# Second-layer products of a soft mixture of experts: four column groups of TensorE per piece in place of two

## The chip, the cores and the metric

The kernel runs on one core of a Trainium2 chip. The metric is the device time of one execution in microseconds. Before the change it is 203.27 us, the median of three runs (203.27 to 203.29).

## The reference

Eight batches of eight heads (576 positions, head dimension 64) pass through an attention with 32 memory slots. The result is laid out as a matrix x of 4608 rows and 512 columns, which goes through a soft mixture of experts with 8 experts of 4 slots each:

```python
logits = x @ phi                                   # 4608 x 32
d = softmax(logits, over rows);  slot_input = d.T @ x     # 32 x 512
for e in range(8):                                 # 4 slots each
    h = maximum(slot_input[e] @ w1[e], 0)          # 4 x 1024
    slot_out[e] = h @ w2[e]                        # 4 x 512
c = softmax(logits, over columns)
out = c @ slot_out                                 # 4608 x 512, float32
```

The weights w1 and w2 are 16.8 MB each, and the output is 9.4 MB. All of it is float32.

## The kernel before

The kernel has two parts. The first, up to about 137 us, does the attention batch by batch, and the logits and the sums of x under their softmax on the way; x itself is never stored. The second part does the experts and writes the output. A planner (the class Plan) takes every group of instructions with a cost in microseconds, a priority and its tiles, simulates the engines and writes out one order for each engine's queue. The order is fixed when the kernel is built; on the chip each engine waits on semaphores only.

**The experts' first layer** (`expert_in`, L1376): for each expert two loads of 1 MB, and 32-column weights (the slot inputs) against 256 columns of w1, put at four positions of the array, `tile_position=(0, NS * j)` with j from 0 to 3 (L1385). `hidden` turns the hidden values round; `hT()[:, x, ...]` then holds them for TensorE's weights, 32 columns per expert of which only its own four are not zero, so that all experts add up in one 32-row block.

**The second layer** (`expert_out` L1439, `mult` L1425): the output's 512 columns are done in two halves, d = 0 and d = 1, each with a bank of PSUM of its own: `pacc[0]` lies in kvbank, `pacc[1]` in scbank. w2 of an expert is laid with eight rows in each partition, and a piece h (0 or 1) is four of them. One call of `mult` does one piece for one half d: four products, each a 32-column weight taken from `hT()[:, 4 * k + x, ...]` against 256 columns of one of the four rows:

```python
for k in range(2):
    for x in range(2 * h, 2 * h + 2):
        nc.tensor.matmul(dst[NS * x: NS * x + NS, :HD], ..., tile_position=(0, NS * x))
```

NS is 32, so x is the column group of the array and also the 32-row block of PSUM in which the product is added. Piece 0 uses groups 0 and 1, piece 1 groups 2 and 3. A float32 product is two instructions (with a weight load each), so that one call of `mult` is 8 matmuls and 8 weight loads. There are 16 pieces and two halves, 32 calls, 256 matmuls. The four blocks of PSUM are four partial sums; `slot_sums` (L1345) copies the bank out (L1349), adds the four blocks with one product against `rep` (L1357), and writes the result `sr` in two parts (L1364, L1369).

**The last five pieces** (the `tails`: piece 1 of expert 5, and both of experts 6 and 7) are loaded apart. `tail_out` (L1471) issues ten loads of 256 KB for the half d = 0 and then ten for d = 1, two for each piece and half. So the half d = 0 is finished while the other's weights are still on their way:

```python
tail_mult(0, n)        # five pieces, half 0, then slot_sums(0)
direct(0, i)           # two output blocks of half 0, before cT is needed
half_group(0, n, ...)  # 16 more blocks of half 0; between them the five tail_mult(1, m)
slot_sums(1), direct(1, i), half_group(1, n), then blocks of both halves
```

Each output block is a product into one of four PSUM banks (L1602; L1586 for the direct ones), a copy out by VectorE (L1579) or ScalarE (L1578), and a store. Stores (L1615) and loads (L502) are all issued by SyncE's queue, in the planner's order: the stores come behind the last load. A store takes one block (128 KB), a group of three (384 KB) or, at the end, 3, 6 and 9 blocks of full width (768, 1536 and 2304 KB). The planner's cost for a call of `mult` is 0.45 us, and it is written as a number where the call is added.

Of the kernel before, what the change touches and what calls it, by code (L numbers as in the profile page):

```python
# [270 lines left out]
def kernel(  # L271
# [27 lines left out]
    E, DM, FF = w1.shape  # L299
    NS = moe_phi.shape[1]  # L300
# [1030 lines left out]
    hT = lambda: hTb.ap.rearrange("p (x y) -> p x y", x=8)  # L1331
# [8 lines left out]
    HD = DM // 2  # L1340
# [4 lines left out]
    def slot_sums(d, middle=lambda: None):  # L1345
        x = slice(d * HD, d * HD + HD)
        add(
            *((ACT, act(HD)) if d else (DVE, dve(HD))),
            lambda: (nc.scalar.copy if d else nc.vector.tensor_copy)(  # L1349
                accs.ap[:, x], pacc[d].ap[:, 0, :HD]  # L1350
            ),
            r=[pacc[d]], w=[accs.part(d)],
        )
        y = middle()
        z = add(
            PE, 0.5,
            lambda: nc.tensor.matmul(  # L1357
                so[d].ap[:, :HD], rep.rearrange("p a n -> p (a n)"), accs.ap[:, x],
                start=True, stop=True,
            ),  # L1360
            r=[accs.part(d), rep_b], w=[so[d]], after=[y] if y is not None else (),
        )
        add(
            ACT, act(HD), lambda: nc.scalar.copy(sr.ap[:, 0, x], so[d].ap[:, :HD]),  # L1364
            r=[so[d]], w=[sr.part(d)],
        )
        add(
            DVE, dve(HD),
            lambda: nc.vector.tensor_tensor(  # L1369
                sr.ap[:, 1, x], so[d].ap[:, :HD], sr.ap[:, 0, x].bitcast(F32), op=ALU.subtract  # L1370
            ),
            r=[so[d], sr.part(d)], w=[sr.part(d)],
        )
        return z
# [50 lines left out]
    def mult(dst, e, h, t, d):  # L1425
        n = 2 if e < ONES else 4
        wide = t.ap.rearrange("p (j t d) -> p j t d", j=n, t=2)
        for k in range(2):
            for x in range(2 * h, 2 * h + 2):
                nc.tensor.matmul(  # L1430
                    dst[NS * x: NS * x + NS, :HD],
                    hT()[:, 4 * k + x, NS * e: NS * e + NS],
                    wide[:, x % n, k, d * HD: d * HD + HD],
                    start=(e == 0 and k == 0),
                    stop=(e == E - 1 and k == 1),
                    tile_position=(0, NS * x),
                )

    def expert_out(e):  # L1439
        w2v = w2[e].rearrange("(p x) d -> p (x d)", x=8)  # L1440
        if e < ONES:
            for h in range(2):
                t = load_w(w2v[:, h * W_SZ: h * W_SZ + W_SZ])
                for d in range(2):
                    add(
                        PE, (0.45, 16),
                        lambda d=d, h=h, t=t: mult(pacc[d].ap[:, 0], e, h, t, d),
                        r=[hTb.part(e // EG), t], w=[pacc[d]],
                    )
            return  # L1450
# [9 lines left out]
        for h in range(2):  # L1460
            if h not in whole:
                tails.append((e, h, t))
                continue
            for d in range(2):
                add(
                    PE, (0.45, 16),
                    lambda d=d, h=h: mult(pacc[d].ap[:, 0], e, h, t, d),
                    r=[hTb.part(e // EG), *(t.part(4 * h + i) for i in range(4))], w=[pacc[d]],
                )
# [13 lines left out]
    def tail_mult(d, n, after=()):  # L1483
        e, h, t = tails[n]
        return add(
            PE, (0.45, 16), lambda: mult(pacc[d].ap[:, 0], e, h, t, d),
            r=[hTb.part(e // EG), *(t.part(4 * h + 2 * d + i) for i in range(2))],
            w=[pacc[d]], after=after,
        )
# [92 lines left out]
    def direct(d, i, after=()):  # L1582
        po, ot, s = b_o.tile(), half[0], slice(d * HD, d * HD + HD)
        x = add(
            PE, 0.45,
            lambda: nc.tensor.matmul(  # L1586
                po.ap[:, :HD], c4.ap[:, i * P: i * P + P], accs.ap[:, s],
                start=True, stop=True,
            ),
            r=[accs.part(d), c4], w=[po], also=[ot], after=after,  # L1590
        )
        add(
            *evict(lambda: ot.ap[:, i * DM + s.start: i * DM + s.stop], po, HD, i % 2 == d),
            r=[po], w=[ot.part(G * d + i)],
        )
        store(0, i, s, ot, [ot.part(G * d + i)], i)
        return x
# [47 lines left out]
    for n in range(-1, NA):  # L1645
# [5 lines left out]
        if RIGHT[NT - 1] == n:  # L1651
            y = slot_sums(1)
            for i in range(ND):
                y = direct(1, i, [y])
# [47 lines left out]
```

## Time and profile before

| what | value |
|---|---|
| median of three runs | 203.27 us |
| the profiled execution | 203.85 us |
| its span, first to last instruction | 202.1 us |
| mean granted clock of TensorE | 0.967 |
| TensorE busy | 171.5 us (85%) |
| VectorE, ScalarE, GpSimd busy | 141.0, 74.7, 95.6 us |
| DMA | 76.47 MB, mean 378 GB/s |
| L1430 (the products of `mult`), kvbank / scbank | 15.1 / 15.5 us busy, 128 matmuls each |

The profile is that of one execution, which took 203.85 us; 1.75 us of it lie outside the span. PE is TensorE's matmuls and PEld its weight loads, DVE is VectorE, ACT ScalarE, POOL GpSimd, SPq the queue of SyncE that issues the DMAs. Times in rows are microseconds from the start of the span, durations in the tables by line are nanoseconds. Ends of matmuls are modelled, and two that overlap are both counted from start to end.

### The profile page before, as it was taken

To read this page: it belongs to the slowest core of one execution; us is meant where nothing else is said; L and a number is where in the kernel's file an instruction comes from. 1 tells how busy PE (TensorE), PEld (TensorE's weight loads), DVE (VectorE), ACT (ScalarE), POOL (GpSimd) and SP (SyncE) were. 2 spreads that over 40 slices of the span, in tenths; PEclk is the share of its full clock that TensorE was granted. 3 is DMA by queue.
4 is the path that set the end of the run, shared out by engine and by line. 5 is a ranking of instruction groups with operands and counts; after the bars stand their busy time and mean duration, and the time that the engine had idled before them with its cause. 6 is when DMAs were issued, how large, how long until landed. Compare 5 with 4: busy or idle time off the path is not lost.

```text
span 202.1 us, 6096 instructions
## 1 busy us (share of the span) xinstructions
PE 171.5 (85%) x2607; PEld 110.2 (55%) x2607; DVE 141.0 (70%) x267; ACT 74.7 (37%) x191; POOL 95.6 (47%) x92
## 2 busy tenths in 40 slices
PE   7889748978789899798999788899999998999910
PEld 6667535545557386465575356565555653557500
DVE  6831640499899899999899996478999502448820
ACT  2022314526361755607373252100347301246600
POOL 7199203479994994799944284000036920000000
PEclk9999996699999999999999999999999999999985
DMA  6999999999999999999999999999999999689996
GB/s 198 363 395 391 383 385 389 383 388 381 401 360 390 385 385 402 381 399 399 417 412 418 417 420 422 420 420 438 425 415 407 342 335 331 224 299 301 393 431 292
DMA packets 31642, 76.47 MB, mean 378 GB/s; under 512 B 2048, under 2 KB 15872, under 8 KB 28288
## 3 DMA queue, kind: packets, MB, share of 16 engines
q1 hardware_dynamic: 31616, 76.09, 99.3%
q8 instruction: 20, 0.33, 0.7%
q14 instruction: 6, 0.05, 0.1%
HBM read 66.65 MB, written 9.44 MB: 377 GB/s over the span
## 4 chain that ended last, share of the span: by engine, by line
PE 38%; DMA 20%; POOL 16%; DVE 10%; issue 6%; SPq 4%; ACT 2%; POOLq 0%; DVEq 0%
DMA arena<-in_moe_w_dram 12%; DMA arena<-in_v_dram 8%; PE bank L1602 7%; PE scbank L813 5%; PE kvbank L704 4%; POOL arena L669 4%; POOL arena L871 4%; SPq L502 4%; PE bank L882 4%; POOL arena L848 4%; PE bank L1385 3%; POOL arena L648 3%; PE scbank L1430 2%; PE bank L1010 2%; DVE arena L827 1%
## 5 line engine op out<-in xcount | busy, mean ns | idle before, releaser
L648 POOL TENSOR_TENSOR arena<-arena 128x1152 f32<-128x1152 f32 x8 | 21.0, 2632 | 16.4 <-ACT arena L641 14.1
L591 DVE STREAM_TRANSPOSE arena<-top 128x1152 f32<-128x1152 f32 x16 | 21.6, 1355 | 8.5 <-DMA top<-in_q_dram 8.5
L704 PE MATMUL kvbank<-arena 64*32 64x128 f32 x1152 | 20.6, 273 | 6.4 <-issue 2.6
L520 PE MATMUL kvbank<-ones 128*128 128x256 f32 x82 | 23.2, 419 | 2.4 <-ACT arena L728 1.3
L813 PE MATMUL scbank<-arena 64*64 64x288 f32 x256 | 23.4, 440 | 2.0 <-DVE arena L827 2.0
L669 POOL TENSOR_TENSOR arena<-arena 128x128 f32<-128x128 f32 (+2 forms) x32 | 23.4, 731 | 3.2 <-ACT arena L657 1.3
L1540 POOL TENSOR_TENSOR cT<-cS,cT 32x640 fp32r<-32x640 f32 (+1 forms) x8 | 11.3, 1413 | 26.2 <-ACT cT L1535 25.8
L871 POOL TENSOR_TENSOR arena<-arena,ssm 128x576 f32<-128x576 f32 x16 | 18.3, 1152 | 10.0 <-DVE ssm L867 7.9
L848 POOL TENSOR_TENSOR arena<-arena,smx 128x576 f32<-128x576 f32 x16 | 18.4, 1153 | 8.1 <-DVE smx L843 8.1
L704 PEld LDWEIGHTS kvbank<-arena 64*32 64x32 f32 x1152 | 16.1, 105 | 10.7 <-issue 5.5
L606 DVE TENSOR_REDUCE arena<-arena 128x128 f32<-128x1152 f32 x8 | 17.1, 2152 | 4.4 <-DMA arena<-in_phi_dram 4.4
L882 PE MATMUL bank<-arena 128*128 128x288 f32 x64 | 18.6, 423 | 1.0 <-DVE arena L874 0.8
L1579 DVE COPY arena<-bank 128x256 f32<-128x256 f32 (+1 forms) x30 | 14.4, 510 | 7.0 <-PE bank L1602 6.4
L520 PEld LDWEIGHTS kvbank<-ones 128*128 128x128 f32 x82 | 15.6, 205 | 5.9 <-ACT arena L728 1.7
L827 DVE STREAM_TRANSPOSE arena<-scbank 128x576 f32<-128x576 f32 x16 | 12.3, 766 | 6.7 <-PE scbank L813 6.7
L1602 PE MATMUL bank<-sr,cT 64*128 64x256 f32 (+1 forms) x100 | 15.1, 358 | 0.5 <-ACT arena L1578 0.2
L1430 PE MATMUL scbank<-arena 128*32 128x256 f32 x128 | 15.5, 381 | 0.0
L1430 PE MATMUL kvbank<-arena 128*32 128x256 f32 x128 | 15.1, 384 | 0.4 <-DMA arena<-in_moe_w_dram 0.2
L813 PEld LDWEIGHTS scbank<-arena 64*64 64x64 f32 x256 | 9.8, 141 | 10.0 <-DVE arena L827 3.3
L853 ACT ACTIVATE arena<-arena 128x576 f32<-128x576 f32 x16 | 10.9, 684 | 10.2 <-POOL arena L848 10.0
L882 PEld LDWEIGHTS bank<-arena 128*128 128x128 f32 x64 | 11.2, 189 | 5.9 <-issue 1.7
L1578 ACT COPY arena<-bank 128x256 f32<-128x256 f32 (+1 forms) x24 | 10.4, 445 | 9.9 <-PE bank L1602 9.0
(135 smaller groups left out, 271.3 us busy)
## 6 DMA issues: line engine op xcount, KB each, us to landing
arena<-in_moe_w_dram SPq DMA_DIRECT2D x19, 1024.0 KB, 14.0
top<-in_q_dram SPq DMA_DIRECT2D x8, 1152.0 KB, 11.6
arena<-in_k_dram SPq DMA_DIRECT2D x8, 1152.0 KB, 10.4
arena<-in_v_dram SPq DMA_DIRECT2D x8, 1152.0 KB, 12.9
arena<-in_moe_w_dram SPq DMA_DIRECT2D x3, 2048.0 KB, 14.2
arena<-in_moe_w_dram SPq DMA_DIRECT2D x20, 256.0 KB, 6.1
arena<-in_phi_dram SPq DMA_DIRECT2D x8, 576.0 KB, 7.2
out_dram<-arena SPq DMA_DIRECT2D x10, 384.0 KB, 4.0
```

The lines of the kernel that those rows point to most:

```text
L520: lambda: nc.tensor.matmul(warm.ap, ones, ones.unsqueeze(1).to_broadcast([P, 2, P]), start=True, stop=True,),
L591: lambda: nc.vector.transpose(qT.ap.rearrange("p (i u y) -> p u i y", i=2, y=Y), qt.ap[:, h * QT_SZ: h * QT_SZ + QT_SZ].rearrange("p (u i ...
L606: lambda: nc.vector.tensor_reduce(mx.ap[:, c0:c1], ph().rearrange("p c j m -> p c m j"), axis=AX.X, op=ALU.max),
L648: lambda: nc.gpsimd.tensor_tensor(ph(), ph(), mb.ap[:, c0:c1].unsqueeze(2).to_broadcast([P, c1 - c0, J, M]), op=ALU.subtract,),
L669: plus = lambda o, x, y: nc.gpsimd.tensor_tensor(o, x, y, op=ALU.add)
L704: nc.tensor.matmul(acc.ap[M * c: M * c + M, a, : 2 * D], ph()[h0: h0 + HALF, c, j, :], kv()[h0: h0 + HALF, :, c, j * D: j * D + D], start= ...
L813: nc.tensor.matmul(scb.ap[HALF * g: HALF * g + HALF, a, :JY], pair[g].kd.ap[h0: h0 + HALF, i, c].rearrange("p r m -> p (r m)"), pair[g].qT ...
L848: lambda: nc.gpsimd.tensor_tensor(exv(), exv(), bc(mx), op=ALU.subtract),
L871: lambda: nc.gpsimd.tensor_tensor(exv(), exv(), bc(sm), op=ALU.mult),
L882: nc.tensor.matmul(lp.ap[:, :JY], vpb.ap[:, h, :], aT.ap[:, a * JY: (a + 1) * JY], start=(h == 0), stop=(h == H - 1),)
L1430: nc.tensor.matmul(dst[NS * x: NS * x + NS, :HD], hT()[:, 4 * k + x, NS * e: NS * e + NS], wide[:, x % n, k, d * HD: d * HD + HD], start=( ...
L1602: nc.tensor.matmul(po.ap[:, : x.stop - x.start], cT[bp].ap[y: y + HALF, j // 2 * P: j // 2 * P + P], sr.ap[y: y + HALF, t, x], start=(t == 0),
```

## The change

In `mult` the two loops exchange the roles of the column groups. The column group is now x = 2k + j, and the piece's own index is y = 2h + j, which still picks the weights and the row of w2. So the four products of one call go to the four groups 0, 1, 2, 3, whatever the piece, where before they went to 0, 1, 0, 1 (piece 0) or 2, 3, 2, 3 (piece 1). Every product, its operands, and the order of the calls stay the same; only the block of PSUM to which a product is added differs, and `slot_sums` adds the blocks as before. The flags that begin and end an accumulation move from k to h, since each block is now met first by piece 0 of expert 0 and last by piece 1 of expert 7.

```diff
         for k in range(2):
-            for x in range(2 * h, 2 * h + 2):
+            for j in range(2):
+                x, y = 2 * k + j, 2 * h + j
                 nc.tensor.matmul(
                     dst[NS * x: NS * x + NS, :HD],
-                    hT()[:, 4 * k + x, NS * e: NS * e + NS],
-                    wide[:, x % n, k, d * HD: d * HD + HD],
-                    start=(e == 0 and k == 0),
-                    stop=(e == E - 1 and k == 1),
+                    hT()[:, 4 * k + y, NS * e: NS * e + NS],
+                    wide[:, y % n, k, d * HD: d * HD + HD],
+                    start=(e == 0 and h == 0),
+                    stop=(e == E - 1 and h == 1),
                     tile_position=(0, NS * x),
                 )
```

## Rows read from the trace of the kernel before

**Rows 1.** By stretch: length; busy PE, PEld, DVE, ACT, POOL; clock, DMA share, GB/s.

```profile
160.00:168.00 8.00, 7.62 (x110) 4.08 (x103) 0.00 (x0) 0.23 (x1) 3.00 (x3) 1.00 1.02 332
168.00:173.00 5.00, 4.48 (x34) 2.51 (x32) 1.97 (x5) 1.39 (x4) 0.00 (x0) 1.00 1.01 330
173.00:184.00 11.00, 10.74 (x84) 6.55 (x81) 5.87 (x16) 4.29 (x12) 0.00 (x0) 1.00 0.74 249
184.00:200.50 16.50, 8.27 (x46) 5.06 (x45) 7.74 (x14) 5.82 (x11) 0.00 (x0) 0.85 1.02 402
```

**Rows 2.** Chain that ended last, from 161 us: start, length, what.

```profile
161.55 6.13 DMA arena<-in_moe_w_dram
167.72 1.06 PE kvbank L1430 x6
...
170.85 0.99 PE scbank L1430 x8
...
172.52 0.99 PE scbank L1430 x8
...
173.93 0.99 PE scbank L1430 x8
...
177.97 0.99 PE scbank L1430 x8
...
192.55 0.69 DVE arena L1579
```

**Rows 3.** SyncE's DMA issues: ten last loads; one store; the last store.

```profile
L502 SPq DMA_DIRECT2D arena<-in_moe_w_dram x10: 368/368/1365, 162.2 to 169.2; - x10
DMA to landing us min/median/max: 5.4/5.6/6.2
...
L1615 SPq DMA_DIRECT2D out_dram<-arena x1: 383/383/383, 175.9 to 175.9; - x1
...
L1615 SPq DMA_DIRECT2D out_dram<-arena x1: 333/333/333, 193.3 to 193.3; - x1
DMA to landing us min/median/max: 7.9/7.9/7.9
```

**Rows 4.** TensorE in order of time: start, length, operation, count.

```profile
136.86 7.06 PEld L1385 LDWEIGHTS bank<-arena,SIM 128*32 128x32 f32 x128 [0.61 <-DVE SIM L1264]
145.65 1.13 PE L1385 MATMUL bank<-top,SIM 128*32 128x256 f32 x16
157.20 0.39 PE L1430 MATMUL scbank<-arena 128*32 128x256 f32 x2
157.24 0.39 PE L1430 MATMUL kvbank<-arena 128*32 128x256 f32 x2
157.42 0.39 PE L1430 MATMUL scbank<-arena 128*32 128x256 f32 x2
170.78 1.06 PE L1430 MATMUL scbank<-arena 128*32 128x256 f32 x8
```

**Rows 5.** Line L1430 alone: one weight load, ns min/median/max.

```profile
L1430 PEld LDWEIGHTS kvbank<-arena x128: 106/109/110, 151.9 to 168.2; 128*32 128x32 f32 x128
```

**Rows 6.** DMA in half microseconds: length, clock, DMA share, GB/s.

```profile
175.50:176.00 0.50, 1.00 0.12 41
...
176.50:177.00 0.50, 1.00 0.29 102
```

**Rows 7.** Granted clock early in the span; columns as in rows 1.

```profile
28.30:30.80 2.50, 0.00 (x0) 0.00 (x0) 1.83 (x1) 0.00 (x0) 0.00 (x0) 1.00 1.05 388
31.75:38.50 6.75, 6.30 (x42) 3.75 (x45) 1.83 (x3) 3.73 (x10) 2.62 (x1) 0.50 1.07 384
54.70:56.00 1.30, 0.19 (x2) 0.10 (x1) 1.06 (x4) 1.14 (x4) 1.30 (x2) 1.00 0.98 336
```

**Rows 8.** Chain of waits: one group of L813 at either clock; columns as in rows 2.

```profile
34.16 2.69 PE scbank L813 x15
...
65.29 1.18 PE scbank L813 x16
```

## The prediction

> **What bounds the kernel now.** I read three views in this order: busy time by stretch, for which stage is short of what; the chain that ended last, for what holds the end; and TensorE's instructions in order of time, for what one call of `mult` costs.
>
> By stretch [rows 1], the DMA engines are full from 160 to 173 us (shares 1.02 and 1.01) and again from 184 to 200.5 (1.02). Between them, from 173 to 184, their share is 0.74, and there TensorE is busy for 10.74 of 11 us. So this is the one late stretch in which TensorE, and not the transfers, sets the pace: the weights have arrived, and the output blocks are not yet made fast enough to fill the engines.
>
> The chain [rows 2] says the same. A load ends its wait at 167.7; then comes the rest of the last piece of half 0 (six matmuls, 1.06 us), and five times a whole call for half 1 with 0.99 us each, of which the first three and the last stand in the rows, among the output blocks. The chain ends with a copy at 192.55, behind which the last store is issued at 193.3 and lands 7.9 us later [rows 3]: it moves 2.3 MB and queues behind what is still under way. So the end is TensorE's pace before 184 us and a full queue after it.
>
> **What a call costs, before and after.** A call is 8 matmuls. Alone on the array, on two column groups, it takes 1.06 us from first start to last end, and the work behind it starts 0.99 us after it [rows 2, 4]. On one column group, matmuls follow each other every 0.215 us: a pair of scbank starts at 157.20 and the next pair at 157.42 [rows 4]. The call puts four on each of its two groups, so it lasts four such rounds.
>
> Four groups can run at once: between those two starts a pair for kvbank starts at 157.24, and it belongs to the next piece, on the other two groups, so that 4 matmuls pass in 0.215 us [rows 4]. The first layer, which uses all four groups in its inner loop, does 16 matmuls, also four rounds, in 1.13 us [rows 4]. After the change a call is two rounds on four groups. Two rounds less than the first layer's 16 are 1.13 - 2 x 0.215 = 0.70 us; two rounds less than today's call are 1.06 - 0.43 = 0.63. The saving of a call that stands alone is thus 0.36 to 0.43 us. I take 0.40, the middle; the rows allow nothing below zero, since each group gets fewer matmuls and their number is the same.
>
> A weight load takes 0.109 us [rows 5]. The Trainium skill, "TensorE: Matmul & The Clock Gate", section "Part 3: Packing small matmuls — row/col tiling", says that a weight load overlaps matmuls in flight only when their row groups differ; here all use all rows. By that rule eight loads would stand one behind the other, a call would not go below its present length, and the time would stay. This case's trace speaks against it: 128 weight loads of the first layer, all of them on all rows, took 7.06 us together, where end to end they would have taken 14.
>
> **Where the saving counts.** There are 32 calls.
>
> 1. The 22 calls of the first eleven pieces (both halves, about 152 to 164 us) mostly overlap already, as the rows at 157 us show: consecutive pieces use different groups. They gain little, perhaps 1 us at the places where two calls with the same groups meet. All of it is lost again in the wait for the last weights: the engines are full up to 173 us whatever TensorE does, and the last load of half 0 ends its wait at 167.7 [rows 1, 2]. Cost and gain at the end: none. If a piece were late behind its data, the wait at 167.7 would not stand in the chain.
>
> 2. The last call of half 0. Two matmuls run when the first of its two loads has landed, six after the second. Today these are four on one group and two on the other, so four rounds. After it they are two on each of three groups, so two rounds: 0.40 us on the chain, between the load and the copy L1349.
>
> 3. The five calls of half 1 that stand in the chain, each between output products that use all columns and can't overlap with it: 5 x 0.40 = 2.0 us.
>
> Half 1's weights must not be late instead. Ten loads issued from 162.2 to 169.2 land within 5.4 to 6.2 us [rows 3], the last at about 174.7; they are evenly spaced by some 0.8 us, so the pairs are complete at about 169, 170.5, 172, 173.3 and 174.7. The first three calls and the last start today at 170.85, 172.52, 173.93 and 177.97 by the chain [rows 2], and by the sum above they would start 0.40, 0.80, 1.20 and 2.00 us earlier: at 170.4, 171.7, 172.7 and 176.0. The nearest margin is that of the third, 0.7 us. The copies out of PSUM don't become the bound either: from 173 to 184 us VectorE is busy for 5.87 and ScalarE for 4.29 of 11 us [rows 1], and would be so in about 9.
>
> Sum on TensorE: 6 x 0.40 = 2.4 us earlier from the first block of half 1 on (bounds 6 x 0.36 = 2.2 and 6 x 0.43 = 2.6). All later copies and the issues of the stores move with it, and the last store would be issued at 190.9 in place of 193.3.
>
> **What the queue of stores makes of it.** From 184 us on the engines are full, so issuing earlier helps only as far as the engines have holes before. Against the full share of 1.02 the 11 us at 0.74 hold 11 x (1 - 0.74 / 1.02) = 3.0 us of holes. The largest lies between 175.5 and 177 us (shares 0.12 and 0.29 in its first and last half microsecond), before the bytes of the store issued at 175.9 [rows 3, 6]: a start-up of about 1 us. Behind three calls of half 1 and the last of half 0, that store is issued 1.6 us earlier, at 174.3, and its bytes start at about 175.3, when those before it end. The stores of half 0 that follow come 1.6 to 2.4 us earlier and leave no hole. The first three of half 1 are single blocks of 128 KB (0.4 us each at the 330 GB/s of rows 1) issued some 0.5 us apart, and leave some 0.5 us of holes. So about 3.0 - 0.5 = 2.5 us of engine time are won, while TensorE gives 2.4: two limits near each other, each of them of a sum with holes in it. When I follow the stores one by one, with a fixed time from the last byte to the landing, I get 2.0. I take 2.2 us.
>
> The profiled execution would end at 203.85 - 2.2 = 201.65 us (its span at 199.9); it stands 0.58 us above the median, so the median would be 203.27 - 2.2 = 201.1 us. The case's own range is 200.7 (2.6 us, TensorE's upper bound) to 201.6 (1.7 us).
>
> **The rivals.**
>
> A. The holes are not the late stores' but the engines' own, or the first stores get in each other's way: the bytes then start late after an earlier issue as well, and only the part after 177 us is won, 3.0 less the 1.2 us of the large hole and 0.6 for the rest, some 1.2 us. Time: 202.1. For it: the engines are idle at 175.5 to 177, though the store before it, of half 0 too, had been issued when its bytes could follow the loads at once. Against it: the hole ends 1 us after an issue.
>
> B. The four groups don't run at once here, because two of the four products now share neither weights nor rows of w2 (in the first layer, four groups share one weight); a call keeps its four rounds, as by the skill's rule above. Time: 203.3. Against it: the overlap at 157 us is between just such products.
>
> C. The slower side: the clock. Faster calls leave TensorE waiting for the last weights of half 0, from about 162.5 to 168 us. With five calls of 0.65 us spread over these waits it is busy for some 60%, against 7.62 of 8 us today [rows 1]. Early in the span the granted clock fell from 1.00 to 0.50, that is from 2.4 to 1.2 GHz, after 2.5 us without a matmul, and then stayed there for 6.75 us [rows 7]; the same group of L813 took 2.69 us in it and 1.18 us at full clock [rows 8]. Such a fall at 168 us would cost about half of the low stretch, 3.4 us, against the 2.4 won: 1.0 us later, 204.3. [...]
>
> **How the numbers follow.** Forecast 0.72, A 0.15, B 0.07, C 0.06. The range reaches from 200.6, just past TensorE's bound, to 202.5, which takes in A and leaves out B and C (0.13) and the edges. A measurement of this kernel tells 0.2% (0.4 us) from no change. Faster: the forecast and A, 0.87. Same: B, 0.07. Slower: C, 0.06.
>
> **What would show it.** In the profile after, a call of half 1 standing alone takes 0.63 to 0.70 us in place of 1.06 (if it is 1.0, B); the chain has 0.55 to 0.65 us for each in place of 0.99; the copy L1349 of half 0 starts near 168.4 and the last store is issued near 190.9 (if these hold and the end moves by much less, A); the share of the DMA engines from 173 to 182 us rises from 0.74 to above 0.9; the clock stays at 1.00 until the last product (if not, C). The prediction is wrong as a whole if the weights of half 1 are waited for, which I have at 0.7 us of margin, or if the output blocks turn out to wait for their copies.

## The result and the profile after

The changed kernel takes 200.94 us (median of four runs, 200.49 to 201.16) against 203.28 us for the kernel before, run beside it. The ratio is 0.9877, with a 95% interval of 0.9855 to 0.9899. Later, on another occasion, the two stood at 200.89 and 203.27 us (0.9883, 0.9867 to 0.9899). The change saves 2.3 us; 2.2 us and 201.1 us were forecast.

Of the two profiled executions, the one before took 203.85 us, 0.57 above its median, and the one after 200.49, 0.45 below. They lie 3.4 us apart, so about 1 us between these two traces is not the change, and below it is kept apart.

The chain that ended last, of the kernel after, from 161 us; its rows answer to [rows 2]. Line 1430 of the kernel before is now 1431, 1602 is 1603.

```profile
161.25 5.52 DMA arena<-in_moe_w_dram
166.77 0.04 issue
166.81 0.67 PE kvbank L1431 x6
...
169.54 0.57 PE scbank L1431 x8
170.11 0.67 PE bank L1603 x8
170.78 0.57 PE scbank L1431 x8
...
171.78 0.57 PE scbank L1431 x8
...
173.74 0.57 PE scbank L1431 x8
...
174.99 0.61 PE scbank L1431 x8
...
189.17 0.69 DVE arena L1580
```

The chain passes through the same instructions, but for one step: behind the last call of half 1 it now goes through the copy L1349 (0.38 us) where it went through four output products (0.43). Its last call of half 0 is 0.67 us long where it was 1.06; the five calls of half 1 are four times 0.57 and once 0.61 where they were 0.99. That is 0.39 and 4 x 0.42 + 0.38 = 2.06 us, together 2.45. The last copy begins at 189.17 in place of 192.55, 3.38 us earlier: 2.45 from the six calls, and 0.91 because the last load of half 0 ended its wait at 166.77 in this execution, where it did at 167.68 in the other.

A second profiled execution of the changed kernel (the run after_again below) took 200.93 us, close to its median. There the load ended its wait at 167.24, and the last copy begins 2.91 us earlier than before, 0.44 of it from the load and 2.47 from the calls:

```profile
161.74 5.50 DMA arena<-in_moe_w_dram
...
189.64 0.69 DVE arena L1580
```

TensorE in order of time, of the kernel after: one call of half 1, and the products that follow it.

```profile
169.47 0.64 PE L1431 MATMUL scbank<-arena 128*32 128x256 f32 x8
170.04 0.39 PE L1603 MATMUL bank<-sr,cT 64*128 64x256 f32 x2
```

The call lasts 0.64 us from first start to last end, against 1.06 [rows 4]: two rounds of 0.215 less, 0.63, was the lower of the two estimates.

Busy time by stretch, of the kernel after; the columns are those of [rows 1].

```profile
160.00:168.00 8.00, 7.07 (x77) 2.42 (x69) 0.42 (x1) 0.00 (x0) 2.71 (x2) 1.00 0.97 316
168.00:173.00 5.00, 5.00 (x48) 2.87 (x48) 2.17 (x6) 1.57 (x5) 0.00 (x0) 1.00 1.07 351
173.00:184.00 11.00, 10.64 (x84) 7.28 (x84) 7.82 (x19) 6.39 (x17) 0.00 (x0) 1.00 1.01 344
```

From 173 to 184 us the share of the DMA engines has risen from 0.74 to 1.01. In this execution the holes are gone but for one at 176.5 to 177 us:

```profile
176.50:177.00 0.50, 1.00 0.60 207
```

The second execution has more of them. Its share is 0.98, which against the full 1.02 leaves 11 x (1 - 0.98 / 1.02) = 0.4 us of holes:

```profile
173.00:184.00 11.00, 10.63 (x86) 7.40 (x86) 7.66 (x19) 6.28 (x17) 0.00 (x0) 1.00 0.98 329
```

And the last store, of which the kernel before has its row in [rows 3], of the kernel after:

```profile
L1616 SPq DMA_DIRECT2D out_dram<-arena x1: 333/333/333, 189.9 to 189.9; - x1
DMA to landing us min/median/max: 8.0/8.0/8.0
```

It is issued 3.4 us earlier and waits and moves for 8.0 us where it took 7.9, so the end moves by as much as TensorE did.

### The profile page after: what moved, and what is told of

It reads as the page before. It is cut to its first block, busy times and chain, and to the rows that moved or that the text cites. A ratio compares the mean times of both kernels' runs of the same rounds, so it can differ in the third digit from the quotient of the medians.

```text
span 198.7 us, 6096 instructions
## 1 busy us (share of the span) xinstructions
PE 168.9 (85%) x2607; PEld 107.7 (54%) x2607; DVE 141.5 (71%) x267; ACT 74.4 (37%) x191; POOL 95.5 (48%) x92
## 4 chain that ended last, share of the span: by engine, by line
PE 37%; DMA 20%; DVE 14%; POOL 12%; issue 4%; SPq 4%; ACT 3%; DVEq 0%; POOLq 0%
DMA arena<-in_moe_w_dram 12%; DMA arena<-in_v_dram 9%; PE bank L1603 6%; PE scbank L813 6%; PE kvbank L704 5%; PE bank L882 4%; SPq L502 4%; POOL arena L848 3%; PE bank L1385 3%; POOL arena L871 3%; POOL arena L669 3%; POOL arena L648 3%; PE bank L1010 2%; DVE arena L606 2%; DVE arena L827 2%
## 5 line engine op out<-in xcount | busy, mean ns | idle before, releaser
L813 PE MATMUL scbank<-arena 64*64 64x288 f32 x256 | 23.6, 445 | 2.3 <-DVE arena L827 2.3
L813 PEld LDWEIGHTS scbank<-arena 64*64 64x64 f32 x256 | 10.0, 141 | 10.1 <-DVE arena L827 3.7
L1603 PEld LDWEIGHTS bank<-sr,cT 64*128 64x128 f32 x100 | 9.9, 184 | 6.5 <-DVE arena L1580 4.1
L1385 PE MATMUL bank<-arena,SIM 128*32 128x256 f32 x224 | 13.3, 392 | 0.2 <-DVE SIM L1264 0.2
```

What stands on the lines that cost most here:

```text
L813: nc.tensor.matmul(scb.ap[HALF * g: HALF * g + HALF, a, :JY], pair[g].kd.ap[h0: h0 + HALF, i, c].rearrange("p r m -> p (r m)"), pair[g].qT ...
L1385: nc.tensor.matmul(hb.ap[NS * j: NS * j + NS, :256], SIM.ap[:, 2 * i + c, NS * e: NS * e + NS], wv[:, c].rearrange("p (x j t) -> p x j t", ...
L1603: nc.tensor.matmul(po.ap[:, : x.stop - x.start], cT[bp].ap[y: y + HALF, j // 2 * P: j // 2 * P + P], sr.ap[y: y + HALF, t, x], start=(t == 0),
```

## The experiments

All times are medians beside runs of the kernel before on the same chip; ratios are to that kernel.

**Where the saving counts.** Four kernels use the four column groups in some of the calls only, and the old two in the others. They differ in one condition, and the flags that begin and end an accumulation follow it:

```diff
+        new = 2 * e + h >= 2 * E - NT and d == 1     # half1_only: five calls
+        new = 2 * e + h >= 2 * E - NT and d == 0     # half0_only: five calls
+        new = 2 * e + h < 2 * E - NT                 # main_only: the 22 others
+        new = 2 * e + h >= 2 * E - NT                # tails_only: ten calls
...
+                y = 2 * h + j
+                x = 2 * k + j if new else y
```

> Only the five calls of half 1 that stand between the output blocks use four column groups; the other 27 are as before. By the theory (each of them is 0.4 us shorter on the chain, and the holes of the store queue take it up): five times 0.42, about 2.1 us faster than before, 201.2. By the rival that a part of the gain comes from the earlier stage (in the profile after, the wait for the last load of half 0 ends 0.9 us earlier): not more than 1.5 us, 201.8 or later.

Measured: 201.44 us against 203.35, ratio 0.992 (0.9901 to 0.9938). The gain is 1.9 us by the medians and 1.6 (1.3 to 2.0) by the ratio. It is somewhat under the 2.1 expected, and the interval does not quite reach that; it takes in the rival's 1.5 as well, so this run alone does not decide between them, but most of the gain is here.

> Only the five calls of half 0 for the last five pieces use four column groups. By the theory only the last of them is on the chain: 0.4 us faster than before, 202.9. By the rival of the earlier stage: 0.4 and whatever comes with an earlier last load, up to 1.3 us, 202.0.

Measured: 202.91 us against 203.35, ratio 0.9981 (0.9973 to 0.999): 0.4 us, as the one call on the chain predicts.

> Only the 22 calls of the first eleven pieces use four column groups; the ten calls of the last five pieces are as before. By the theory the transfers set this stage: no change, 203.3, and the last load of half 0 ends its wait where it did. By the rival of the earlier stage: 0.9 us faster, 202.4.

Measured: 203.30 us against 203.35, ratio 0.9999 (0.999 to 1.0009). Twenty-two of the 32 calls, changed alone, are worth nothing. In the chain of this kernel the wait for a load still stands before the last call of half 0:

```profile
161.54 5.62 DMA arena<-in_moe_w_dram
167.17 0.04 issue
167.21 1.06 PE kvbank L1433 x6
```

The rival's 0.9 us is outside the interval of this run (0.2 us either way). The three gains by medians are 1.9, 0.4 and 0.05 us and add up to 2.4, against 2.3 for all calls at once.

Whether the 22 calls matter once the ten later ones are short was then tried by the counterpart, beside the kernel after.

> Only the ten calls of the last five pieces (both halves) use four column groups; the 22 earlier calls are as before. By the theory (the earlier stage waits for its weights either way): as the kernel after on the same chip, within 0.2 us. By the rival that the earlier calls matter once the later ones are short (in two profiles with the earlier calls as before, the chain ran through TensorE from 160 us on, without a wait for a load): 0.3 to 0.5 us slower than the kernel after.

> The kernel after, unchanged, timed beside tails_only on the same chip: 200.9 by both theories, 2.0 to 2.5 us less than the kernel before.

Measured: tails_only 200.99 us, ratio 0.9888 (0.9871 to 0.9906); the kernel after 200.89, ratio 0.9883 (0.9867 to 0.9899); before 203.27. There is no difference that can be told: the ten calls do all of it, as far as 0.2 us can be told.

**How much the store queue lets through.** Two kernels leave out the five calls of half 1 for the last five pieces, before and after the change, and keep everything else in its place (the flags that end an accumulation follow). What TensorE no longer does there is 5 x 0.99 and 5 x 0.57 us.

```diff
     def mult(dst, e, h, t, d):
+        if d == 1 and 2 * e + h >= 2 * E - NT:
+            return
```

> The kernel before, with the five calls of half 1 for the last five pieces left out (their share of the output's right half is missing); loads, order and stores stay. TensorE gets 5 x 0.99 = 4.95 us. By the theory of two limits the holes of the store queue (3.0 us) cap the gain: 2.5 to 3.0 us, 200.3 to 200.8, with the DMA share full from 173 us on. By the rival that TensorE alone sets the end: 4.95 us, 198.3.

Measured: 201.05 us against 203.35, ratio 0.99 (0.9879 to 0.9921): 2.3 us by medians, 1.6 to 2.5 by the interval, out of TensorE's 4.95. TensorE alone is refuted, and the cap stands somewhat lower than the 2.5 to 3.0 us expected.

> The kernel after, with the five calls of half 1 for the last five pieces left out (their share of the output's right half is missing); loads, order and stores stay. TensorE gets another 5 x 0.57 = 2.85 us. By the theory that the store queue is now full (holes of some 0.3 us are left from 173 us on): at most 0.3 us faster than the kernel after, 200.6 to 200.9. By the rival that TensorE still sets the end: 2.85 us faster than it, 198.1.

Measured: 200.48 us against 203.44, ratio 0.9832 (0.978 to 0.9884). That is 0.4 us less than the kernel after in its own runs (200.89 and 200.94, on other occasions), for 2.85 us less work. Against the kernel before, each beside its own runs, it is 3.0 us where the kernel after has 2.4, so 0.6. The runs spread from 199.97 to 201.1, so neither figure is sharp, but 198.1 is far off.

Not all of the time left out reaches the end of TensorE's work either. From the end of the direct blocks to the product against `rep` for half 1, the chain takes 8.58 us in the kernel before and 4.53 in before_skip, 4.05 less and not 4.95; in the kernel after it takes 6.51 and in after_skip 4.52, 1.99 less and not 2.85. Without the calls the output blocks wait for more of their copies: in after_skip a copy by VectorE (0.42 us) stands in the chain that did not stand there in the kernel after. The product is shown for before, after and after_skip, the last with the two copies ahead of it:

```profile
179.43 0.70 PE kvbank L1357 x2
```

```profile
176.05 0.70 PE kvbank L1357 x2
```

```profile
170.00 2.04 PE bank L1605 x14
...
172.60 0.36 ACT arena L1581
...
173.56 0.42 DVE arena L1582
...
174.52 0.63 PE kvbank L1357 x2
```

The last store of these two kernels tells how the rest was given back: before_skip first, after_skip second.

```profile
L1617 SPq DMA_DIRECT2D out_dram<-arena x1: 333/333/333, 188.5 to 188.5; - x1
DMA to landing us min/median/max: 9.5/9.5/9.5
```

```profile
L1618 SPq DMA_DIRECT2D out_dram<-arena x1: 332/332/332, 188.4 to 188.4; - x1
DMA to landing us min/median/max: 9.2/9.2/9.2
```

Against the kernel after the last store of before_skip is issued 1.4 us earlier and takes 1.5 us longer to land, 198.0 in place of 197.9. It stands in a queue that is full from 168 us on (before_skip, columns as in [rows 1]):

```profile
168.00:173.00 5.00, 4.39 (x29) 3.33 (x28) 3.37 (x9) 2.15 (x7) 0.00 (x0) 1.00 1.07 353
173.00:184.00 11.00, 10.35 (x67) 7.44 (x69) 8.23 (x19) 6.97 (x18) 0.00 (x0) 1.00 1.03 352
```

**Whether a call is a number of rounds.** If the groups set the length, putting all four products of a call on one of them must nearly double it against the kernel before: eight rounds in place of four.

```diff
-                x, y = 2 * k + j, 2 * h + j
+                y = 2 * h + j
+                x = 0 if d == 1 and 2 * e + h >= 2 * E - NT else 2 * k + j
```

> The kernel after, with all four products of the five half-1 calls of the last pieces put on one column group. By the theory of rounds (matmuls of one group follow each other every 0.215 us, whatever else is free) such a call has eight rounds, 8 x 0.215 + 0.2 = 1.9 us, 1.28 more on the chain than after: 5 x 1.28 = 6.4 us of TensorE, less nothing, as the queue has no holes to give: 207.3 from 200.9. By the rival that a group could take its matmuls faster when it has more of them in a row (weights loaded behind the matmul, 0.11 us each): 1.06 a call, as in the kernel before, 202.9.

Measured: 207.32 us against 203.44, ratio 1.0165 (1.0114 to 1.0216). The forecast was 207.3. In its chain the call is 1.84 us, after 0.57 on four groups and 0.99 on two, so 0.42 us for each pair of rounds over the whole scale:

```profile
170.19 1.84 PE scbank L1432 x8
172.03 0.67 PE bank L1607 x8
172.70 1.84 PE scbank L1432 x8
```

Here TensorE sets the end and the queue waits for it. The DMA share from 173 to 184 us is 0.50:

```profile
173.00:184.00 11.00, 10.75 (x61) 5.78 (x59) 3.04 (x8) 2.46 (x8) 0.00 (x0) 1.00 0.50 167
```

**Two attempts to use the full queue.** If the queue is the limit, fewer slow bytes should help. In the kernel after, the stores in halves (rows of 1 KB) move at 344 GB/s from 173 to 184 us, and the long rows of the last stores at 435 from 187 to 195:

```profile
187.00:195.00 8.00, 2.13 (x11) 1.00 (x10) 2.44 (x4) 1.76 (x3) 0.00 (x0) 0.84 1.03 435
```

```diff
-    NT, NA = 5, 6
+    NT, NA = 5, 5                # na5; one more full-width store, of three blocks, ahead of the last three
+    NT, NA = 4, 6                # nt4; RIGHT = (-1, 1, 1, 2)
```

> The kernel after, with five groups of three blocks written in halves in place of six; the sixth is written in full width, ahead of the last three stores. If the store queue is the limit now, what counts is how fast it moves: 0.79 MB go from about 345 GB/s (rows of 1 KB) to about 420 (rows of 6 KB), 2.3 - 1.9 = 0.4 us: 200.5. By the rival that TensorE or the copies set the end: no change from after, 200.9.

Measured: 201.59 us against 203.44, ratio 0.9893 (0.9848 to 0.9939). The gain of 0.4 us over the kernel after did not come. By medians it is 0.7 us worse, and 0.5 worse when each is set against its own runs of the kernel before, though the intervals overlap. Its trace shows new holes (share 0.73, 0.73 and 0.40 in three single microseconds):

```profile
174.00:175.00 1.00, 0.98 (x10) 0.45 (x10) 0.82 (x3) 0.25 (x1) 0.00 (x0) 1.00 0.73 253
177.00:178.00 1.00, 1.00 (x6) 0.87 (x5) 0.05 (x1) 0.37 (x1) 0.00 (x0) 1.00 0.73 253
179.00:180.00 1.00, 1.00 (x9) 0.65 (x10) 0.83 (x3) 0.78 (x3) 0.00 (x0) 1.00 0.40 138
```

A likely reason, which no run tests: the group that now goes out in full width had been what the engines moved while TensorE finished half 1.

> The kernel after, with four pieces loaded apart in place of five; the fifth piece comes with the rest of its expert in one load of 2 MB. Four loads of 256 KB (about 330 GB/s) become part of a large one (about 410): 1.05 MB, 3.2 - 2.55 = 0.6 us of queue time less, but the half 0 is complete about 1 us later and the loads that cover its first blocks end sooner. By the theory of the full queue without new holes: 200.3. With a hole of 0.5 us or so before the second group's store: 200.8. By the rival that the output blocks' start sets the end: 1 us later, less 0.57 for the call that goes, 201.4.

Measured: 201.95 us against 203.44, ratio 0.9912 (0.9882 to 0.9942): 0.5 us past the rival's 201.4, and 1.0 us above the kernel after by medians. Its DMA share from 168 to 173 us is 0.96 and from 173 to 184 us 0.94, where the kernel after has 1.07 and 1.01. How much of this is the later start and how much the shorter cover was not taken apart. Neither attempt beat the kernel after.

## Why the prediction was right

1. **The bound.** From 173 to 184 us TensorE set the pace, and a full queue did after it. one_group and before_skip show both sides. Slower calls move the end by their whole length: 6.4 us for 5 x 1.27. Calls that are left out move it by 2.3 us, where they are 4.95 us long and TensorE's chain became 4.05 shorter.

2. **A call's length.** 0.40 us saved was the term, 0.38 to 0.42 was measured, and the same step of 0.42 holds between one group and two. Rival B, that two unrelated products don't run at once, is refuted by the 0.64 us of a call. So is, for this case, the rule of the Trainium skill ("TensorE: Matmul & The Clock Gate", "Part 3: Packing small matmuls — row/col tiling") that the prediction sets beside it, that a weight load overlaps matmuls in flight only when their row groups differ: in a call of 0.64 us, loads that all use the same rows did not wait for matmuls on other column groups.

3. **Which calls count.** Six of 32 were forecast: 2.4 us, where the chain after gives 2.45. The 22 earlier ones were put at nothing, and main_only and tails_only measure that. No call of half 1 waited for its load, so the margin of 0.7 us held. The signs that were named by their time came early: the copy L1349 began at 167.50 and 167.97 in the two profiled executions in place of 168.4, and the last store was issued at 189.9 and 190.4 in place of 190.9. The prediction took the end of the load's wait, 167.7, from an execution that was above the median, and it varies from run to run. The cover named, the wait for the last weights, is thin, though. In the profiled execution of half0_only (203.36 us, above its median) TensorE counts as busy from 160 to 168 us without a break, and the chain ran through it and not through a load; so it did in those of half1_only and before_skip, which are below their medians. Of half0_only:

```profile
165.98 2.31 PE kvbank L1433 x38
168.29 0.02 issue
```

In such an execution the earlier calls could count; over the runs they didn't.

4. **The queue.** The forecast had two limits close together, 2.4 us from TensorE and 2.5 from the holes. It left 0.5 us of holes in its sum; 0.4 us were left in one execution and 0.2 in the other (half a microsecond at 0.60). The queue took all that TensorE gave, and little more would have fitted: without the five calls the last store was issued 1.5 to 2.0 us earlier still, and the medians gained 0.4 to 0.6. Rival A, in which the large hole stays, is refuted by the shares of 1.01 and 0.98. The store-by-store working, which gave 2.0 us, held too much back; taking 2.2 between it and the 2.4 was a compromise and not a mechanism, so that the forecast lies within 0.2 us of the measured 2.3 to 2.4 is in part luck.

5. **The clock.** It stayed at 1.00 in all three stretches. TensorE counts as busy for 4.57 of 5.5 us (83%) between 162.5 and 168 us, where rival C put some 60%: a piece's matmuls run in two bursts, one behind each of its two loads (at 163.4 and 164.1 us for one of them), and not as one call of 0.65 us.

```profile
162.50:168.00 5.50, 4.57 (x33) 1.04 (x31) 0.42 (x1) 0.00 (x0) 0.28 (x1) 1.00 0.98 319
```

Rival C did not come about, but no run tests how near it was. The 2.5 us without a matmul that it reads from [rows 7] is not a safe measure: at the end of the second profiled execution the last matmul ended at 189.6 us, and the granted clock was 0.72 on the mean from 190 to 191 us already.

```profile
190.00:191.00 1.00, 0.00 (x0) 0.72 1.07 455
```

## What to carry to other kernels

Count how many matmuls of a burst fall on each column group: when groups are free, the length of a burst that stands alone goes by the fullest group, not by the number of matmuls. Bursts that follow each other on different groups overlap already, and bursts that wait for their data gain nothing, so look for the few that stand alone on the chain. Before a saving is booked there, add up the holes of the queue behind it: the smaller of the two is what arrives. Once both were used up here, leaving calls out brought a fraction of their length, and the two attempts with fewer slow bytes brought nothing.

## What the runs showed of the hardware that was not expected

By their recorded starts, matmuls did not start in program order when their column groups differed. In the code of the kernel before, a whole call for scbank stands ahead of the next piece's call for kvbank, yet the latter's pairs start between the former's (157.20, 157.24, 157.42 in [rows 4]); so calls overlapped that in the code stand one behind the other. And a DMA's time to landing is no measure of its size: the same last store took 7.9, 8.0, 9.2 and 9.5 us as it was issued at 193.3, 189.9, 188.4 and 188.5 (before, after, after_skip, before_skip).
